# Filling products of a constant in place of identity transpositions, at the start of a clustered-attention and two-MLP kernel

## The chip, the cores and the metric

The kernel runs on one core of one Trainium2 chip. The metric is device time in microseconds (us) for one execution, lower being better. Before the change three runs took 782.43, 779.1 and 779.32 us: a median of 779.32 us. A further execution was recorded by the hardware profiler; the rows below come from that one.

## The reference

Three stages follow each other, all in float32. The first is attention in which a query sees only the keys of its own cluster; its output goes through one MLP with softplus, and that through a gated one with silu.

```python
q_assign = argmax(einsum('bhsd,hcd->bhsc', q_n, c_n), -1)   # q_n, k_n, c_n: normalised
k_assign = argmax(einsum('bhsd,hcd->bhsc', k_n, c_n), -1)
mask = q_assign[:, :, :, None] == k_assign[:, :, None, :]
scores = where(mask, q @ k.T / sqrt(D), -1e9)
x = softmax(scores) @ v            # B 2, H 8, S 768, D 64, 16 clusters
x = softplus(x @ w_in) @ w_out     # 1536 tokens, 512 -> 2048 -> 512
return (silu(x @ w_gate) * (x @ w_val)) @ w_out2    # 512 -> 1536 -> 512
```

The filling products that the change is about are no part of this: their result is never read.

## The kernel before, in words

Heads are taken in pairs; the 16 pieces of batch and head give 8 pairs, and each head has 6 blocks of 128 queries. One block is one step of the main loop: scores into PSUM (`sc`, L589), the row maximum on VectorE (L597), the exponential on ScalarE (L605), six transpositions of the probabilities on TensorE (`tr`, L621), their split into a high part (ScalarE, L627) and a low part (VectorE, L628), and the products with v (`pv`, L638). After the attention come the two MLPs (L914, L1092, L1185, L1435), nearly all of it TensorE work.

Ahead of the loop stands a prologue, written out by hand for the first pair. Each engine works off its own queue in the order in which the program issues it, so the order of the code is the order of the work:

- q and k of the first pair come in four pieces (`qkn`, L376), two halves each, on the queues of SP and ScalarE; the centroids (`cnc`) on SP's.
- TensorE has nothing to do until the first piece lands. It is filled with work whose result nobody reads: two products of a 128 x 128 tile of ones with itself (L390), then `warm(9)`, nine transpositions of the identity `id32` (L387). The identity is built by GpSimd (masks.py:197 and 199).
- `prep_x` (L455) transposes a half of q or k, three 128 x 128 transpositions; ScalarE or VectorE copies the result out (L463, L460, L465). The order on TensorE is: q half 0, `warm(1)`, k half 0, the centroids' transposition `cps` (L431), `warm(1)`, q half 1.
- `sims0` (L719) then multiplies the transposed q and k with the centroids `C`, 12 products with only 32 moving columns in two groups of six for each half; VectorE finds the cluster of each row (`arg0`, L732 to L737).
- The same is done for q of the next pair (`prep_x` L455, `sims_tile` L497), the cluster numbers are transposed (`hot_t`, L787), and the first scores are made (L589).

All of the filling writes the tile `warm_ps`, which is 128 columns of the PSUM bank with the tag "o". `prep_x` of q half 1 takes that bank next, so it waits until the last filling transposition is out of TensorE's pipeline.

The lines that the change touches:

```python
    warm_ps = ps_o.tile([128, 512], F32, tag="o", name="warm")[:, 0:128]
    ones = nc.const_aps.tensor(1.0, [128, 128], F32)

    def warm(n):
        for _ in range(n):
            nc.tensor.transpose(warm_ps, id32, id32)

    for _ in range(2):
        nc.tensor.matmul(warm_ps, lhsT=ones, rhs=ones, start=True, stop=True)
    warm(9)
```

Of the kernel before, what the change touches and what calls it, by code (L numbers as in the profile page):

```python
# [41 lines left out]
def kernel(  # L42
# [18 lines left out]
    nc = tc.nc  # L61
# [29 lines left out]
    id32 = keep.tile([128, 128], F32, name="id32")  # L91
# [290 lines left out]
    warm_ps = ps_o.tile([128, 512], F32, tag="o", name="warm")[:, 0:128]  # L382
    ones = nc.const_aps.tensor(1.0, [128, 128], F32)

    def warm(n):
        for _ in range(n):
            nc.tensor.transpose(warm_ps, id32, id32)  # L387

    for _ in range(2):
        nc.tensor.matmul(warm_ps, lhsT=ones, rhs=ones, start=True, stop=True)  # L390
    warm(9)

    nc.vector.tensor_copy(idr, id32)
    ohs = sml.tile([4 * C, 2], F32, name="ohs", bufs=1)
# [361 lines left out]
    bank_from(ps_t, "t")  # L756
    prep_x(0, 0, 0)
    warm(1)
    prep_x(0, 1, 0)
    centroid_blocks()  # L760
    warm(1)
    high0(0, 0)
    bank_from(ps_o, "o")
# [862 lines left out]
```

## Time and profile before

| | before |
|---|---|
| median of three runs | 779.32 us |
| the profiled execution's own time | 785.12 us |
| its span, first to last instruction | 783.3 us |
| TensorE busy (products / weight loads) | 779.0 / 714.4 us |
| VectorE, ScalarE, GpSimd busy | 614.0, 492.4, 171.2 us |
| granted TensorE clock, mean of the span | 0.991 |

A product's row in the timeline is a group of neighbouring instructions: start, time from the first one's start to the last one's end, engine, line, what it writes and reads, and how many. PE is the products, PEld the loads of the stationary operand ahead of them. A float32 product is two records in the trace, with a load each (two products of ones appear as x4); a float32 transposition is one. The time of one record contains the way through the pipeline, so records overlap: the step from one record to the next is (time of the group - time of its last record) / (count - 1). "Granted clock" is the share of TensorE's full 2.4 GHz that its throttle let through: 1.00 is 2.4 GHz and 0.50 is 1.2 GHz.

### The profile page before, as it was taken

The page shows a single profiled execution, that of the slowest core. Times are in us where ns is not written, and L with a number is a line of the kernel's source. Part 1 is how long each engine was busy: PE and PEld are TensorE (multiplying, and loading weights), DVE is VectorE, ACT ScalarE, POOL GpSimd, SP SyncE. Part 2 cuts the span into 40 slices and gives each one's busy share as a digit, 9 for nine tenths or more (in the row PEclk, how much of TensorE's full clock was granted, in tenths as well). Part 3 has the DMA queues.
Part 4 walks back from the last instruction along what each step waited for, and adds up shares of the span by engine and source line. Part 5 has one row for each costly group of instructions (what it writes and reads, how often), then busy time and mean ns, then how long its engine had stood idle before and what let it go on. Part 6 is the DMA issues. An engine that isn't in the chain of part 4 may idle for free.

```text
span 783.3 us, 12198 instructions
## 1 busy us (share of the span) xinstructions
PE 779.0 (99%) x4542; PEld 714.4 (91%) x4542; DVE 614.0 (78%) x988; ACT 492.4 (63%) x893; POOL 171.2 (22%) x174
## 2 busy tenths in 40 slices
PE   9999999999999999999999999999999999999998
PEld 9999999999999888889889898899999999999996
DVE  5899988988998798888776777998756766665664
ACT  5889889889897465447456465366564555555430
POOL 9545556556533000100100100000001011101100
PEclk7999999999999999999999999999999999999999
DMA  8784864864611323725736525113336567667554
GB/s 204 202 216 127 207 159 123 190 156 122 144 32 48 112 81 107 189 55 133 142 104 131 111 78 188 54 63 99 123 147 139 121 143 154 142 115 151 87 185 162
DMA packets 72652, 102.80 MB, mean 131 GB/s; under 512 B 29808, under 2 KB 52688, under 8 KB 72592
## 3 DMA queue, kind: packets, MB, share of 16 engines
q1 hardware_dynamic: 66608, 82.94, 36.1%
q0 software_dynamic: 5184, 18.88, 15.9%
q8 instruction: 36, 0.59, 0.3%
q10 hardware_dynamic: 800, 0.20, 0.1%
q14 instruction: 24, 0.20, 0.1%
HBM read 52.99 MB, written 26.79 MB: 102 GB/s over the span
## 4 chain that ended last, share of the span: by engine, by line
PE 93%; DVE 4%; ACT 1%; DMA 1%; issue 0%; SPq 0%; DVEq 0%
PE x L1185 17%; PE ob L1092 17%; PE ob L1435 12%; PE w L1185 9%; PE sps L589 8%; PE ops L638 8%; PE tps L621 8%; PE bank L914 5%; PE y L1185 4%; PE sims L497 2%; PE mps L455 2%; DVE tl L628 1%; DMA R<-rd 1%; DVE gl L1010 0%; ACT th L627 0%; PE mps L555 0%
## 5 line engine op out<-in xcount | busy, mean ns | idle before, releaser
L628 DVE TENSOR_TENSOR tl<-tps,th 128x384 fp32r<-128x384 f32 x192 | 98.1, 550 | 8.6 <-ACT th L627 7.5
L597 DVE TENSOR_REDUCE nm<-sps 128x1 f32<-128x768 f32 x96 | 91.2, 950 | 12.5 <-PE sps L589 10.7
L627 ACT CAST th<-tps 128x384 fp32r<-128x384 f32 x192 | 84.7, 491 | 16.4 <-PE tps L621 13.2
L621 PE MATMUL tps<-id,p 128*128 128x128 f32 x576 | 92.4, 280 | 0.1
L605 ACT ACTIVATE p<-sps,nm 128x768 f32<-128x768 f32 x96 | 88.1, 918 | 2.9 <-DVE nm L597 2.9
L589 PE MATMUL sps<-KT,QT 128*128 128x384 f32 x384 | 85.5, 345 | 0.0
L621 PEld LDWEIGHTS tps<-id,p 128*128 128x128 f32 x576 | 74.4, 150 | 8.0 <-DVE tl L628 3.5
L638 PE MATMUL ops<-th,VV 128*128 128x256 f32 x288 | 80.0, 307 | 0.0
L1452 POOL DMA_DIRECT2D out_dram<-side x21 | 18.1, 863 | 275.5 <-ACT side L1448 275.5
L638 PE MATMUL ops<-tl,VV 128*128 128x256 f32 x288 | 72.6, 282 | 0.0
L589 PEld LDWEIGHTS sps<-KT,QT 128*128 128x128 f32 x384 | 64.8, 194 | 0.0
L1435 PE MATMUL ob<-whi,aa 128*128 128x512 f32 x168 | 56.7, 391 | 0.0
L175 DVE TENSOR_TENSOR wlo<-m,whi 128x512 fp32r<-128x512 f32 (+1 forms) x63 | 38.6, 625 | 21.4 <-ACT whi L170 21.1
L638 PEld LDWEIGHTS ops<-th,VV 128*128 128x128 f32 x288 | 54.4, 189 | 0.4 <-DVE xu L659 0.2
L638 PEld LDWEIGHTS ops<-tl,VV 128*128 128x128 f32 x288 | 54.7, 190 | 0.0
L1118 POOL DMA_DIRECT2D far_acc<-side x15 | 13.1, 870 | 189.0 <-ACT side L1113 189.0
L170 ACT CAST whi<-m 128x512 fp32r<-128x512 f32 (+1 forms) x62 | 34.0, 561 | 29.5 <-DVE m L154 29.4
L1092 PE MATMUL ob<-gl,whi 128*128 128x512 f32 x168 | 51.9, 390 | 0.1
L1092 PE MATMUL ob<-gh,whi 128*128 128x512 f32 x168 | 51.8, 390 | 0.0
L1092 PE MATMUL ob<-gh,wlo 128*128 128x512 f32 x168 | 51.8, 389 | 0.0
L175 DVE TENSOR_TENSOR wlo<-side,whi 128x512 fp32r<-128x512 f32 x30 | 20.7, 692 | 31.6 <-ACT whi L170 31.5
L154 DVE SCALAR_TENSOR_TENSOR m<-raw,m 128x512 int32<-128x512 int32 x68 | 44.7, 686 | 0.7
(281 smaller groups left out, 1973.4 us busy)
## 6 DMA issues: line engine op xcount, KB each, us to landing
raw<-in_moe_w_out_dram SPq DMA_DIRECT2D x28, 512.0 KB, 4.4
out_dram<-side POOLq DMA_DIRECT2D x21, 512.0 KB, 5.6
raw<-in_moe_w_in_dram SPq DMA_DIRECT2D x16, 512.0 KB, 4.4
far_acc<-side POOLq DMA_DIRECT2D x15, 512.0 KB, 6.0
raw<-in_moe_w_gate_dram SPq DMA_DIRECT2D x12, 512.0 KB, 3.5
raw<-in_moe_w_val_dram SPq DMA_DIRECT2D x12, 512.0 KB, 4.2
QT<-hi SPq DMA_DIRECT2D x30, 192.0 KB, 3.5
KT<-hi SPq DMA_DIRECT2D x14, 384.0 KB, 6.0
```

Of the source, the lines that this page charges most:

```text
L154: nc.vector.scalar_tensor_tensor(out=m, in0=lo, scalar=29, in1=m, op0=ALU.logical_shift_right, op1=ALU.bitwise_or)
L175: low()
L589: nc.tensor.matmul(ps[:, c, 0:384], lhsT=Q[:, a, 128 * j:128 * j + 128], rhs=K[:, a, 384 * c:384 * c + 384], start=(a == 1), stop=(a == 0),)
L597: nc.vector.tensor_reduce(out=nm, in_=ps[:, :, 0:384], axis=AX.XY, op=ALU.max, negate=True)
L605: nc.scalar.activation(out=_h(p), in_=s_t.pop(i)[:, :, 0:384], func=AF.Exp, bias=nm_t.pop(i), accum_out=sm_t[pr][:, j:j + 1],)
L621: nc.tensor.transpose(ps[:, 128 * j:128 * j + 128], p[:, 128 * kb:128 * kb + 128], id32)
L627: nc.scalar.copy(th, pv)
L628: nc.vector.tensor_tensor(out=tl, in0=pv, in1=_r(th), op=ALU.subtract)
L638: nc.tensor.matmul(o[:, 0:CW], lhsT=VV_t[pr][:, hh, kb].rearrange("p a d -> p (a d)"), rhs=t[:, kb, :], start=(kb == 0 and lohi == 0), sto ...
L1092: nc.tensor.matmul(bk[:, t, :], lhsT=wt[:, 0, 128 * d:128 * d + 128], rhs=gt[:, 512 * c:512 * c + 512], start=(ends[0] and ff == 0 and n = ...
L1185: nc.tensor.matmul(dst[:, c, :], lhsT=wt[:, at + kk, :], rhs=x(part, kk)[:, HT // 2 * c:HT // 2 * c + HT // 2], start=(first and kk == 0 a ...
L1435: nc.tensor.matmul(bk[:, t, :], lhsT=lhs[:, ts_], rhs=rhs[:, 0, :], start=(ff == 0 and i == 0), stop=(ff == 1 and i == 2),)
```

## The change

The two products of ones and the nine identity transpositions become 12 products of the same tile of ones with 64 of its columns, and `warm(1)`, which is called twice between the transpositions of q and k, becomes one such product each time. The stationary operand keeps its 128 columns; the moving one has 64 instead of 128. Everything behind moves up two lines in the code.

```diff
     def warm(n):
         for _ in range(n):
-            nc.tensor.transpose(warm_ps, id32, id32)
-
-    for _ in range(2):
-        nc.tensor.matmul(warm_ps, lhsT=ones, rhs=ones, start=True, stop=True)
-    warm(9)
+            nc.tensor.matmul(warm_ps[:, 0:64], lhsT=ones, rhs=ones[:, 0:64], start=True, stop=True)
+
+    warm(12)
```

TensorE's queue from its first product to q half 1, before the change (`warm` is the filling, `mps` a transposition of q or k, `cps` that of the centroids; in brackets the semaphores waited for, DMAHW being a landing):

```order
L390 MATMUL warm<-const-float32-1.0 128x128 x2
L387 MATMUL warm<-id_72 128x128 [waits Pool_49]
L387 MATMUL warm<-id_72 128x128 x8
L455 MATMUL mps<-id_72,qkn 128x128 [waits DMAHW2_49,DMAHW0_49]
L455 MATMUL mps<-id_72,qkn 128x128 x2
L387 MATMUL warm<-id_72 128x128
L455 MATMUL mps<-id_72,qkn 128x128 [waits DMAHW4_49,DMAHW3_49]
L455 MATMUL mps<-id_72,qkn 128x128 x2
L431 MATMUL cps<-id_72,cnc_107 64x128 [waits DVE_49]
L387 MATMUL warm<-id_72 128x128
L455 MATMUL mps<-id_72,qkn 128x128 [waits DMAHW6_49,DMAHW5_49,PE_49]
```

Eleven filling instructions stand ahead of the first transposition of q, and the first identity transposition waits for GpSimd. The same stretch of TensorE's queue with the change:

```order
L387 MATMUL warm<-const-float32-1.0 128x64 x12
L453 MATMUL mps<-id_72,qkn 128x128 [waits DMAHW2_49,DMAHW0_49,Pool_49]
L453 MATMUL mps<-id_72,qkn 128x128 x2
L387 MATMUL warm<-const-float32-1.0 128x64
L453 MATMUL mps<-id_72,qkn 128x128 [waits DMAHW4_49,DMAHW3_49]
L453 MATMUL mps<-id_72,qkn 128x128 x2
L429 MATMUL cps<-id_72,cnc_107 64x128 [waits DVE_49]
L387 MATMUL warm<-const-float32-1.0 128x64
L453 MATMUL mps<-id_72,qkn 128x128 [waits DMAHW6_49,DMAHW5_49,PE_49]
```

Twelve products stand there now, and the wait for GpSimd's identity has moved to the first transposition of q. Nothing else in the queue has changed its place.

## Rows read from the trace of the kernel before

**Rows 1.** The page: span, busy time by engine, the chain that ended last by engine.

```profile
span 783.3 us, 12198 instructions
...
PE 779.0 (99%) x4542; PEld 714.4 (91%) x4542; DVE 614.0 (78%) x988; ACT 492.4 (63%) x893; POOL 171.2 (22%) x174
...
PE 93%; DVE 4%; ACT 1%; DMA 1%; issue 0%; SPq 0%; DVEq 0%
```

**Rows 2.** Timeline of the first 24 us, TensorE's rows in part.

```profile
0.79 1.19 PE L390 MATMUL warm<-const-float32-1.0 128*128 128x128 f32 x4 [0.79 <-PEq L1610]
1.77 2.13 PE L387 MATMUL warm<-id 128*128 128x128 f32 x9
...
3.82 0.50 PEld L455 LDWEIGHTS mps<-id,qkn 128*128 128x128 f32 x3 [0.32 <-issue]
...
6.07 0.55 PE L455 MATMUL mps<-id,qkn 128*128 128x128 f32 x3
...
6.45 1.42 PE L719 MATMUL y<-C,xr 128*128 128x32 f32 x12
...
9.59 1.52 PE L455 MATMUL mps<-id,qn 128*128 128x128 f32 x6
...
11.25 2.73 PE L497 MATMUL sims<-C,xr 128*128 128x32 f32 x12
...
18.05 2.60 PE L497 MATMUL sims<-C,xr 128*128 128x32 f32 x12
...
20.46 1.63 PE L589 MATMUL sps<-KT,QT 128*128 128x384 f32 x4
...
28.05 0.82 PE L621 MATMUL tps<-id,p 128*128 128x128 f32 x6
```

**Rows 3.** Instructions of L390, L387, L719, L497, L621: count, ns min/median/max, first and last start.

```profile
L390 PE MATMUL warm<-const-float32-1.0 x4: 421/422/553, 0.8 to 1.6; 128*128 128x128 f32 x4
L387 PE MATMUL warm<-id x11: 421/421/421, 1.8 to 5.6; 128*128 128x128 f32 x11
L719 PE MATMUL y<-C,xr x24: 195/276/389, 6.5 to 9.4; 128*128 128x32 f32 x24
L497 PE MATMUL sims<-C,xr x168: 193/276/402, 11.2 to 201.1; 128*128 128x32 f32 x168
L621 PE MATMUL tps<-id,p x576: 270/272/421, 21.9 to 248.2; 128*128 128x128 f32 x192
```

**Rows 4.** Windows: busy by engine, then granted clock, DMA share, GB/s.

```profile
core 0: us, PE busy (x) PEld busy (x) DVE busy (x) ACT busy (x) POOL busy (x), PEclk, DMA share, GB/s
0.00:6.00 6.00, 5.21 (x22) 4.49 (x22) 2.69 (x16) 2.44 (x5) 5.22 (x28) 1.00 0.62 139
6.00:9.40 3.40, 3.34 (x31) 3.25 (x31) 2.34 (x6) 2.74 (x7) 3.17 (x5) 1.00 0.96 221
9.40:23.06 13.66, 13.66 (x64) 13.47 (x63) 7.29 (x14) 7.17 (x15) 13.15 (x14) 0.50 0.96 264
23.06:26.50 3.44, 3.38 (x21) 2.44 (x20) 3.25 (x7) 3.36 (x9) 0.76 (x1) 1.00 0.94 256
```

**Rows 5.** Who TensorE's weight loads waited for, whole span, and in the first 30 us.

```profile
PEld tps L621 <- DVE tl L628: 3.5, 17, 0.4
...
PEld tps L621 <- DVE tl L628: 1.0, 4, 0.4
```

## The prediction

> **What bounds the kernel now.** I read the page first [rows 1]: TensorE is busy 779.0 of 783.3 us and is 93% of the chain that ended last. Time that TensorE loses anywhere is therefore time of the kernel, unless it waits for another engine soon after. That is nearly never so: its longest wait for one line is 3.5 us, for VectorE's L628, in 17 pieces over the whole span, 1.0 us of it in the first 30 us [rows 5]. So I take a delay at the start as passed through to the end, less what a later wait could swallow, at most 1 us near by.
>
> The change lies in the first 6 us, so I read the timeline there next [rows 2]. The filling starts at 0.79. The nine transpositions start at 1.77 and take 2.13 us with the pipeline's tail; without the last one's tail (421 ns for a record, a step of (2.13 - 0.42) / 8 = 0.213 us) the array is free at 1.77 + 9 x 0.213 = 3.69. The first load for q half 0 comes at 3.82. It waits for landings only, so the data was there at 3.8: **the filling ends 0.13 us before it is in the way.**
>
> Then the clock. The windows give the granted clock as 1.00 until 9.4, 0.50 from there to 23.06, and 1.00 after [rows 4]. The first value is not what ran. An identity transposition took 421 ns from 1.8 to 5.6 us, every one of the 11, and a transposition in L621 took 421 ns at most and 272 ns at the median [rows 3]; its step at 28.05 is (0.82 - 0.27) / 5 = 0.110 us [rows 2], half of 0.213. So TensorE ran at 1.2 GHz until about 6 us. From there the three transpositions at 6.07 fit in 0.55 us and the L719 records took 276 ns, which is 2.4 GHz. Read that way: half speed until 6, full for 3.4 us, half for 13.66 us, then full for good.
>
> What the engine did before each turn is what matters here. Ahead of the rise at 6 it ran 128-column transpositions almost without a gap. Ahead of the fall at 9.4 it ran mostly L719, products of 32 columns. In the half-speed stretch it ran L497 twice, again 32 columns. It rose at 23.06, after the scores at 20.46 and their transpositions, which follow the last L497.
>
> **The change part by part.**
>
> (1) The filling itself. Removed: 4 records of ones and 9 transpositions, 13 steps. Added: 12 products, 24 records of 64 moving columns, each with a weight load of 128 columns. No row shows 64 columns. The rows on both sides do, at 1.2 GHz: ones with 128 columns step by 0.213 us or a little more ((1.19 - 0.42) / 3 = 0.257 with the slow first one), and L497 with 32 columns by (2.73 - 0.40) / 11 = 0.212 [rows 2, 3]. Four times the columns, the same step: at these sizes the step is that of the weight load, which the change leaves as it is. So I take 0.213 for 64 columns. As a lower bound I keep half of it, 0.107, as if columns decided.
> 24 x 0.213 = 5.11, and 0.13 for the slow first record: the filling ends at 0.79 + 5.24 = 6.03 instead of 3.69, and q half 0 starts 6.03 - 3.82 = **2.2 us late**. At the lower bound it ends at 3.5 and costs nothing, the wait for data at 3.82 covering it.
>
> (2) The two single fillings: one record of 0.213 becomes two, **+0.43 us**. The second has no cover: q half 1 waits for the bank it writes. The first loses whatever cover the data of k half 0 gave it; that data has landed when q is 2.2 us late. Lower bound 0.
>
> (3) The wait for GpSimd's identity moves to q half 0. The old first transposition of it began at 1.77 [rows 2], so it is done 2 us ahead of the data: nothing. VectorE, ScalarE and SP have their orders unchanged; what they take from TensorE's first results comes later by the same 2 to 3 us. Behind them GpSimd is busy 13.15 of the 13.66 us from 9.4 [rows 4], but what it makes there (the second head's operands, v) is read by TensorE only from 26.5 on, and TensorE is later too.
>
> (4) The clock. The transpositions that came ahead of the rise at 6 are gone. In their place stand products with half their columns at the same step, so that the array is fed half as densely. 64 columns lie between the 128 ahead of a rise and the 32 ahead of a fall. I take it that the rise at 6 does not come, the nearer likeness being a step that is mostly weight load. Then the work from 6.07 to 9.59 (6 transpositions, 24 records of L719) runs at 1.2 GHz: 30 x 0.213 = 6.4 us instead of 3.5, **+2.9 us**. Lower bound 0, if the rise comes all the same.
> The Trainium skill says the opposite of what I read: in "TensorE: Matmul & The Clock Gate", Part 4, PE-mode transpose, the full clock does not engage for transpositions, as they don't count as busy in the same way. By that rule real products would be the better filling. The trace disagrees here: from 1.77 to 6 TensorE ran nothing but transpositions, and then came the full clock.
>
> (5) What comes back. TensorE reaches the transpositions of 9.59 at 2.2 + 0.4 + 2.9 = 5.5 us late. If the full clock comes at the same moment as before, 23.06, those last 5.5 us of work run at 2.4 GHz: -2.7. If it comes at the same point of the work, nothing comes back. If it comes later in the work, up to the 12 L497 records and 4 score products behind the first dense stretch (2.4 + 1.4 us at half speed), some 2.4 us more are lost with what follows. I see no row that ties it to a moment, and take -0.8, nearer to the same point of the work.
>
> Sum: 2.2 + 0.4 + 2.9 - 0.8 = **+4.7 us**. Made against the profiled execution that is 785.12 + 4.7 = 789.8 with the profiler on. That execution stands 5.8 us above the median of the plain runs, so for a plain run I put the sum on the median: 779.32 + 4.7 = **784.0 us**. The plain runs themselves differ by 3.3 us, which is about what an earlier or later rise of the clock is worth by (5).
>
> **The rivals.**
>
> *Columns decide the step.* 24 records at 0.107 end at 3.5, before the data, as the filling did before. For it: a real product of fewer columns streams less. Against it: 32 and 128 columns have one step in rows 2. Time: 779.3 if the clock rises as before, 779.3 + 2.9 = 782.2 if not. [...]
>
> *Products bring the clock up.* The filling is slow as in (1) until the full clock comes, at 6 or up to 2 us sooner. At 6: q half 0 is 2.2 us late; it, k and the single fillings then run at full speed, 11 steps of 0.110 instead of 0.213, which leaves 1.5 us (2.2 + 0.4 - 1.1) at q half 1; and 1.5 us of L719 is pushed behind the fall at 9.4 and costs as much again: 3.0, so 782.3. Sooner: some 10 of the 24 records at 0.110, so 1.0 less on the filling: about 780. For it: real products ran ahead of the rise at 6, too, from 0.79 to 1.98. Against it: these were four records, the rest transpositions.
>
> *Faster: products bring the clock up and it stays up.* Decided by the granted clock after 9.4: if it stays at 1.00, the 13.66 us of half speed shrink to 6.8 if VectorE and ScalarE, 7.3 and 7.2 us busy there [rows 4], can follow: about -6.5, less 2 us of late filling, 774.8. Against it: L719 and L497 are untouched, and the clock fell during the one and stayed low over the other.
>
> **How the numbers follow.** A measurement of this kernel can tell about 0.5% from no change, 3.9 us here: 775.4 to 783.2 counts as the same. My forecast has a chance of 0.60, with its own range from 781.3 (2.0, the full 2.7 coming back and some of 2 covered) to 787.2 (5.5 and 2.4 more); four fifths of it lie over 783.2, 0.48. Columns decide: 0.14, counted with the same. Products bring the clock up: 0.18, 0.04 of it slower. It stays up: 0.06, faster; 0.02 more for a lucky early rise. Together: faster 0.08, same 0.40, slower 0.52. The range of 778.0 to 787.2 leaves out the faster case and a tenth or so at the top.
>
> **What would show it.** In the profile of the changed kernel: 24 filling records with a step of 0.21 us, ending near 6.0; the first q transposition at 6.0 and not 3.85; L719 with records of about 0.40 us and its first row near 9.2; the first L455 of `qn` near 15 instead of 9.59; no full clock between 6 and 9.4. Wrong in (1) if the first q load still comes at 3.8; wrong in (4) if L719's median stays at 276 ns; wrong as a whole if the clock is up before the first score product.

## The result: slower by 8.6 us, and the profile after

The changed kernel took 787.13, 787.55, 788.16 and 790.38 us, a median of 787.86, against 779.21 before (four runs on the same chip). The ratio is 1.0102, 95% interval 1.0069 to 1.0134: slower, with the whole interval above the 0.5% that the prediction took as telling. The forecast was slower by 4.7 to 784.0 with a range up to 787.2; the way was right, the time lies 0.7 us above the range.

The timeline of the changed kernel's first 29 us, TensorE's rows in part, against [rows 2]:

```profile
0.79 5.35 PE L387 MATMUL warm<-const-float32-1.0 128*128 128x64 f32 x24 [0.79 <-PEq L1608]
5.93 0.85 PE L453 MATMUL mps<-id,qkn 128*128 128x128 f32 x3
6.57 0.53 PE L387 MATMUL warm<-const-float32-1.0 128*128 128x64 f32 x2
6.89 0.85 PE L453 MATMUL mps<-id,qkn 128*128 128x128 f32 x3
...
7.74 0.53 PE L387 MATMUL warm<-const-float32-1.0 128*128 128x64 f32 x2
8.33 0.90 PE L453 MATMUL mps<-id,qkn 128*128 128x128 f32 x3
9.02 2.61 PE L717 MATMUL y<-C,xr 128*128 128x32 f32 x12
...
14.54 1.52 PE L453 MATMUL mps<-id,qn 128*128 128x128 f32 x6
...
16.19 2.73 PE L495 MATMUL sims<-C,xr 128*128 128x32 f32 x12
...
19.65 1.63 PE L587 MATMUL sps<-KT,QT 128*128 128x384 f32 x4
...
21.57 1.20 PE L587 MATMUL sps<-KT,QT 128*128 128x384 f32 x4
22.61 1.42 PE L495 MATMUL sims<-C,xr 128*128 128x32 f32 x12
...
28.89 0.36 PE L636 MATMUL ops<-th,VV 128*128 128x256 f32 x1
```

24 filling records step by (5.35 - 0.42) / 23 = 0.214 us and are through at 5.93, where the first transposition of q now starts instead of 3.85. Twelve L717 records take 2.61 us where they took 1.42, and the `qn` transpositions come at 14.54 instead of 9.59. The first sign of the full clock is inside the group at 21.57: 1.20 us where the same four products took 1.63 at 19.65. The instructions of the two lines say the same:

```profile
L387 PE MATMUL warm<-const-float32-1.0 x28: 314/421/443, 0.8 to 7.8; 128*128 128x64 f32 x28
L717 PE MATMUL y<-C,xr x24: 261/401/401, 9.0 to 14.3; 128*128 128x32 f32 x24
```

The median of L717 is 401 ns after 276 before [rows 3]. The granted clock does not show any of this. The windows of the changed kernel's trace read 1.00 from the start:

```profile
core 0: us, PE busy (x) PEld busy (x) DVE busy (x) ACT busy (x) POOL busy (x), PEclk, DMA share, GB/s
0.00:6.00 6.00, 5.21 (x25) 5.25 (x26) 2.32 (x15) 1.78 (x3) 5.22 (x28) 1.00 0.62 139
6.00:9.40 3.40, 3.34 (x18) 3.12 (x17) 1.41 (x2) 1.55 (x5) 1.36 (x3) 1.00 0.96 218
9.40:22.10 12.70, 12.70 (x62) 12.60 (x62) 5.51 (x13) 6.54 (x13) 10.70 (x12) 1.00 0.69 179
22.10:26.50 4.40, 4.25 (x32) 3.89 (x31) 3.90 (x7) 3.64 (x8) 4.20 (x5) 1.00 0.99 319
```

By the durations TensorE ran at 1.2 GHz for 22 us. The windows before the clock's first turn can't be relied on, then: here, as in the first 6 us of the kernel before [rows 4], they print 1.00 over half speed. A likely reason, not shown, is that nothing is recorded ahead of the first turn. The page still shows a span that is TensorE's from end to end:

```profile
span 786.4 us, 12224 instructions
...
PE 781.2 (99%) x4555; PEld 717.3 (91%) x4555; DVE 614.4 (78%) x988; ACT 493.0 (63%) x893; POOL 171.3 (22%) x174
...
PE 96%; DVE 1%; ACT 1%; DMA 1%; issue 0%
```

One thing does not fit: the span grew by 3.1 us only (783.3 to 786.4), the plain median by 8.6. So the recorded execution of before may not have been one of its usual ones.

### The profile page after: what moved, and what is told of

Its sections match the earlier page's. It is cut to its first block, busy times and chain, and to the rows that moved or that the text cites. A ratio compares the mean times of both kernels' runs of the same rounds, so it can differ in the third digit from the quotient of the medians.

```text
span 786.4 us, 12224 instructions
## 1 busy us (share of the span) xinstructions
PE 781.2 (99%) x4555; PEld 717.3 (91%) x4555; DVE 614.4 (78%) x988; ACT 493.0 (63%) x893; POOL 171.3 (22%) x174
## 4 chain that ended last, share of the span: by engine, by line
PE 96%; DVE 1%; ACT 1%; DMA 1%; issue 0%
PE x L1183 17%; PE ob L1090 17%; PE ob L1433 12%; PE w L1183 8%; PE ops L636 8%; PE sps L587 8%; PE tps L619 8%; PE bank L912 8%; PE y L1183 4%; PE sims L495 2%; PE mps L453 1%; PE bank L936 1%; PE warm L387 1%; DMA QT<-OH 1%; PE y L717 1%; DVE tl L626 0%
## 5 line engine op out<-in xcount | busy, mean ns | idle before, releaser
L625 ACT CAST th<-tps 128x384 fp32r<-128x384 f32 x192 | 84.7, 491 | 14.2 <-PE tps L619 11.5
```

What stands on the lines that cost most here:

```text
L625: nc.scalar.copy(th, pv)
```

## The experiments

The theories. **A**: a float32 filling product steps with its load of stationary columns, so the filling ends 2 us late; and behind these products, with half the moving columns in each step, the full clock does not come up early, as it does behind filling with 128 columns. **Rivals**: only the late filling costs; only real products bring the clock up; columns decide the step; the turns of the clock stand at fixed times. The kernels were timed in three groups, each with before beside it: 77 executions of before, with medians of 779.37, 779.08 and 779.63 us.

**b_again: before once more.** No edit.

> The kernel before, unchanged, with a second profile. Theory A (the turns of the clock do not stand at fixed times after the start, and where they fall makes the 778.7 to 782.4 us of the plain runs): the median is 779 to 782, and the profile shows the rise, the fall and the last rise at other times than 6.0, 9.4 and 23.06 us. Rival B (the turns are fixed, and the profiler itself makes the difference to 785): the three turns are within 0.3 us of those times.

Measured: 779.56 us over 10 executions from 778.74 to 785.84; 1.0007 (0.9975 to 1.0039). The new profile has a span of 777.0:

```profile
4.16 0.59 PE L455 MATMUL mps<-id,qkn 128*128 128x128 f32 x3 [0.26 <-DMA qkn<-in_q_dram]
...
6.00 1.42 PE L719 MATMUL y<-C,xr 128*128 128x32 f32 x12
...
9.04 0.85 PE L455 MATMUL mps<-id,qn 128*128 128x128 f32 x6
...
10.14 1.52 PE L497 MATMUL sims<-C,xr 128*128 128x32 f32 x12
...
12.05 0.98 PE L589 MATMUL sps<-KT,QT 128*128 128x384 f32 x4
...
20.54 0.36 PE L638 MATMUL ops<-th,VV 128*128 128x256 f32 x1
```

Here the 12 records of L497 take 1.52 us and not 2.73 [rows 2]: the full clock came up ahead of 5 us and did not fall at 9.4 at all. The three transpositions at 4.16 already take 0.59 us, where those at half speed take 0.85 or more. The first `pv` product (L638) is at 20.54; in the recorded execution of before it was at 26.54. Rival "fixed times" is out. The recorded execution, with a mean of 0.991, was one of a minority in which the clock falls for a while: the mean granted clock of the ten was 0.989 in the two at 785.5 and 785.8 us, 0.996 in the two at 782.4 and 782.6, and 0.999 or 1.000 in the six at or below 779.8. Of the 77 executions of before, 24 took over 781 us.

**e1_five: five products instead of twelve.**

```diff
-    warm(12)
+    warm(5)
```

> 5 products of 64 columns in place of 12, the single ones as in the change. Theory A: 10 records of 0.213 us end at about 3.0, so q half 0 starts at 3.8 to 3.9 as before the change, but there is no full clock around 6 to 9.4 and L717 has records of 401 ns. Against the change 2.1 us less: about 785.5, and still 4 to 7 above before. Rival B (the late filling alone costs, the clock does not matter): 779 to 780.

Measured: 785.12 us, 1.0071 (1.0056 to 1.0087), 2.7 below the change.

```profile
0.79 2.37 PE L387 MATMUL warm<-const-float32-1.0 128*128 128x64 f32 x10 [0.79 <-PEq L1608]
3.96 0.88 PE L453 MATMUL mps<-id,qkn 128*128 128x128 f32 x3 [0.80 <-DMA qkn<-in_q_dram]
...
7.08 2.61 PE L717 MATMUL y<-C,xr 128*128 128x32 f32 x12
...
19.63 1.13 PE L587 MATMUL sps<-KT,QT 128*128 128x384 f32 x4
```

The filling is over 0.8 us before the data, L717 still runs at half speed, and 5.7 us of the 8.6 are still there. "The late filling alone" is out.

**e2_wide: the change with 128 columns.**

```diff
-            nc.tensor.matmul(warm_ps[:, 0:64], lhsT=ones, rhs=ones[:, 0:64], start=True, stop=True)
+            nc.tensor.matmul(warm_ps, lhsT=ones, rhs=ones, start=True, stop=True)
```

> The change with 128 moving columns in place of 64. Theory A: the step stays 0.213 us, q half 0 starts 1 to 2.2 us late, but the full clock comes at some time up to 7 us and most of L717 has records of 276 ns: 781 to 784. Rival B (what the moving columns are does not matter to the clock): no full clock before 16 us, 787 to 790 as the change. Rival C (columns decide the step): the step is well above 0.213.

Measured: 781.01 us, 1.0015 (1.0005 to 1.0024), all ten from 779.5 to 781.66.

```profile
0.79 5.46 PE L387 MATMUL warm<-const-float32-1.0 128*128 128x128 f32 x24 [0.79 <-PEq L1608]
6.04 0.68 PE L453 MATMUL mps<-id,qkn 128*128 128x128 f32 x3
...
8.04 1.42 PE L717 MATMUL y<-C,xr 128*128 128x32 f32 x12
```

Twice the columns cost 0.1 us: 24 records are through at 6.04 instead of 5.93. So in this row the step is not set by the columns that stream. But L717 runs at full speed behind them. With the filling just as late, the kernel is 1.6 us above before where the clock comes up, and 8.6 where it does not.

**e3_ids: transpositions only.** The filling of before with no product of ones, 21 identity transpositions at the outset and two in each single place.

```diff
-    for _ in range(2):
-        nc.tensor.matmul(warm_ps, lhsT=ones, rhs=ones, start=True, stop=True)
-    warm(9)
+    warm(21)
...
-    warm(1)
+    warm(2)
...
-    warm(1)
+    warm(2)
```

> 21 transpositions of the identity, and two at a time where the change has one product, with no product of ones at all: the filling ends where that of the change does, at about 5.9. Theory A (dense transpositions bring the clock up by themselves): the full clock comes by 7 us, q half 0 at most 2.2 us late, 781 to 784, as with 128 columns. Rival B (only products count, as the Trainium skill has it in TensorE: Matmul & The Clock Gate, Part 4): no full clock before 16 us, 787 to 790.

Measured: 780.93 us, 1.0017 (1.0002 to 1.0032).

```profile
1.37 4.70 PE L387 MATMUL warm<-id 128*128 128x128 f32 x21 [1.37 <-POOL id masks.py:199]
5.91 0.49 PE L453 MATMUL mps<-id,qkn 128*128 128x128 f32 x3
...
7.71 1.42 PE L717 MATMUL y<-C,xr 128*128 128x32 f32 x12
```

Three transpositions in 0.49 us at 5.91: full speed, with nothing but transpositions ahead. The Trainium skill's statement in "TensorE: Matmul & The Clock Gate", Part 4, PE-mode transpose, that the full clock does not engage for them, does not hold for these float32 transpositions; the measurement decides.

**e4_six: six products of 128 columns**, two records in each single place. The edit is that of e2_wide with `warm(6)`.

> Six products of 128 columns ahead of the data, and one such at each of the two single places. Theory A (a filling with 128 columns that ends before the data costs nothing and brings the clock up): 12 records of 0.213 us end at 3.5, q half 0 starts at 3.8 to 4.2, the full clock comes between 4 and 7 us; 778.7 to 780.5. Rival B (real products of a constant bring less than transpositions do): no full clock before 16 us, 784 to 786.

Measured: 779.28 us, 1.0001 (0.9978 to 1.0025).

```profile
0.79 2.90 PE L387 MATMUL warm<-const-float32-1.0 128*128 128x128 f32 x12 [0.79 <-PEq L1608]
3.67 0.56 PE L453 MATMUL mps<-id,qkn 128*128 128x128 f32 x3
...
6.67 1.42 PE L717 MATMUL y<-C,xr 128*128 128x32 f32 x12
```

The 12 records are through when q half 0 starts, at 3.67, and L717 takes 1.42 us. Behind real products of a constant with 128 columns the clock came up here as it does behind the transpositions of before. In one execution of the ten, at 786.14 us, the mean granted clock was 0.991, as in the recorded one of before.

**e5_square: 64 stationary columns too.**

```diff
-            nc.tensor.matmul(warm_ps[:, 0:64], lhsT=ones, rhs=ones[:, 0:64], start=True, stop=True)
+            nc.tensor.matmul(warm_ps[0:64, 0:64], lhsT=ones[:, 0:64], rhs=ones[:, 0:64], start=True, stop=True)
```

> The products of the change with 64 stationary columns as well as 64 moving ones. Theory A (the load of the stationary columns sets the step, and a stream with half the columns in half the step is as dense as before): a step of 0.107 us, 24 records end at 3.4, q half 0 at 3.8 to 4.2, the full clock by 7 us; 778.7 to 781. Rival B (the step is fixed per float32 record, whatever the columns): 0.213 us, q half 0 at 5.9, 787 to 788. Rival C (the step halves but a product of 64 columns does nothing for the clock): q half 0 on time, no full clock before 16 us, 784.5 to 785.5.

Measured: 779.5 us, 1.0018 (0.9988 to 1.0047), seven executions from 778.98 to 779.77 and three from 785.25 to 787.0. The profile caught one of the three:

```profile
0.79 2.79 PE L387 MATMUL warm<-const-float32-1.0 128*64 128x64 f32 x24 [0.79 <-PEq L1608]
3.70 0.87 PE L453 MATMUL mps<-id,qkn 128*128 128x128 f32 x3
...
7.18 2.61 PE L717 MATMUL y<-C,xr 128*128 128x32 f32 x12
```

The step is (2.79 - 0.31) / 23 = 0.108 us, with 314 ns for a record (its median in this trace): half the stationary columns, half the step. With e2_wide this shows that in a long row of such products the stationary columns set the step, not the moving ones. That it is their load, and not something else that goes with them, is the likely reading but was not tested apart. On the clock the kernel is mixed. In seven of ten its time is that of before, so there the clock most likely came up early, though none of the seven was profiled; in the profiled one it did not. So the early rise can come behind products of 64 columns (rival C, as stated, falls), but why in some executions and not in others was not settled.

**e6_none: no filling at all.** All three calls of `warm` are removed.

> No filling at all, neither the 12 products nor the two single ones. Theory A (the filling of the change does nothing for the clock): q half 0 at 3.8 to 4.2, no full clock before 16 us, 784 to 785.5, that is 2.5 to 4 us below the change. Rival B (half as dense a filling is still worth something): above the change or level with it, 787 to 789.

Measured: 784.49 us, 1.0077 (1.005 to 1.0103): 784.08, 784.47, 784.51 and 788.25. The profile is of the last, the one that stands apart:

```profile
3.81 1.53 PE L452 MATMUL mps<-id,qkn 128*128 128x128 f32 x6 [3.81 <-DMA qkn<-in_q_dram]
...
6.41 2.61 PE L716 MATMUL y<-C,xr 128*128 128x32 f32 x12
...
27.92 1.25 PE L586 MATMUL sps<-KT,QT 128*128 128x384 f32 x4
```

q half 0 starts at 3.81, and L716, which is L717 of the change, takes 2.61 us. The full clock comes only inside the group at 27.92 here, which may be what sets this execution apart; the three others have no profile. By the medians the filling of the change is 3.4 us worse than none, or 2.6 with the median of after_again; that of before is 5.4 us better than none.

**e7_single: the two single fillings alone.** The filling of before, with a product of 64 columns in place of each single transposition.

> The filling of the kernel before at the outset, and only the two single transpositions replaced by products of 64 columns. Theory A: at most 0.4 us more than before, 779 to 780, with the full clock by 7 us. Rival B (the two single ones take the clock down): 784 to 786.

Measured: 782.72 us, 1.0037 (1.0013 to 1.0062): neither theory. Six of ten executions were over 781 us, against 5 of the 24 of before beside them. The profile is one of the six; the clock rises near 6 and falls near 9.3, as in the recorded one of before. The first single product costs 0.1 us more than a transposition: k half 0 starts 0.31 us behind it (4.62 to 4.93 in this profile), where the step after a transposition is 0.21. Beside the before of its group the kernel is slower, with an interval that lies above 1. Whether the single products also make the fall more frequent, or whether ten executions are too few, stays open: over all three groups before had 24 of 77.

**after_again: the changed kernel once more.**

> The changed kernel, unchanged, with a second profile. Theory A: the step is 0.213 us again, q half 0 starts at 5.9, and the full clock first comes between 19 and 25 us, wherever it falls in the work; 787 to 790. If the wait of L587 for the transfer QT<-OH (1.1 us in the first profile) belongs to the change, it is there again; if it was chance, it is not, and the time is the same within 1 us or so.

Measured: 787.11 us over nine executions, 781.81 to 789.25; 1.0061 (1.0026 to 1.0096). The filling, L717 and the rise stand as in the first profile within 0.02 us, and the first `pv` product is at 28.88, there 28.89. The first profile also had this row among the waits of TensorE's loads, at the change of a head pair near 106 us:

```profile
PEld sps L587 <- DMA QT<-OH: 1.1, 1, 1.1
```

The second does not have it, and its span is 785.3, just 1.1 less. It is not part of the change. Three of the nine took 781.8 to 784.7 us. None of them was profiled; by their times the full clock came earlier there. So the change most likely does not shut the early rise out in every execution.

**e8_seven and e9_pairs: two tries at a better one.** e8_seven is e4_six with `warm(7)`; e9_pairs is before with `warm(2)` in both single places.

> Seven products of 128 columns instead of six, the single ones as there. Theory A (a filling that reaches up to the data leaves no hole before q half 0, and so loses the full clock in fewer executions): 14 records end at 3.9, at most 0.2 us late; 778.8 to 779.8, and fewer executions above 781 than the kernel before has. Rival B (what decides is where the clock's turns fall, not the hole): the same share of executions above 781, a fifth or so.

> The kernel before with two identity transpositions at each of the two single places. Theory A (denser single fillings hold the full clock through L719 more often): the median 0.1 to 0.4 us above before, 779.1 to 779.8, with fewer executions above 781. Rival B (they only cost): 779.3 to 780 and a fifth of the executions above 781 as before.

Measured: e8_seven 780.35 us, 1.0013 (0.9991 to 1.0036), 4 of 12 over 781 us; e9_pairs 779.3 us, 0.9991 (0.996 to 1.0021), 2 of 12 over 781, with before at 779.63 and 12 of 28. Neither can be told from before. With a third of its executions over 781 us, e8_seven gives no sign of its theory A; the share of e9_pairs goes the way of its own, but 12 executions are too few to show it. No version was found that beats before.

## Why the prediction was right, and where it fell short

Where the lateness builds up, against the usual execution of before (the profile of b_again) and against the recorded one:

| start of | usual before | recorded before | after | late against usual / recorded |
|---|---|---|---|---|
| q half 0 | 4.16 | 3.85 | 5.93 | 1.8 / 2.1 |
| first products with the centroids | 6.00 | 6.45 | 9.02 | 3.0 / 2.6 |
| `qn` transpositions | 9.04 | 9.59 | 14.54 | 5.5 / 5.0 |
| first score product | 12.05 | 14.70 | 19.65 | 7.6 / 5.0 |
| first `pv` product | 20.54 | 26.54 | 28.89 | 8.4 / 2.4 |
| end (span) | 777.0 | 783.3 | 786.4 | 9.4 / 3.1 |

Of the last row 1.1 us is the wait for QT<-OH, which after_again did not have. Rows of the recorded before that the table and the steps rest on, beside [rows 2]:

```profile
3.85 0.87 PE L455 MATMUL mps<-id,qkn 128*128 128x128 f32 x3
4.52 0.42 PE L387 MATMUL warm<-id 128*128 128x128 f32 x1
4.73 0.85 PE L455 MATMUL mps<-id,qkn 128*128 128x128 f32 x3
...
5.59 0.42 PE L387 MATMUL warm<-id 128*128 128x128 f32 x1
...
14.70 1.63 PE L589 MATMUL sps<-KT,QT 128*128 128x384 f32 x4
...
26.54 0.36 PE L638 MATMUL ops<-th,VV 128*128 128x256 f32 x1
```

- Step (1), the filling: right. 0.213 us was taken for a record, 0.214 was measured; the end at 6.03 was forecast, 5.93 measured (the first record was less slow). e2_wide and e5_square bear out the reason given: the stationary columns set the step.
- Step (2), +0.43 for the single ones: half of that. The pair at 6.57 puts k half 0 0.32 us behind its start, where one transposition at 4.52 put it 0.21 behind; the second place takes 0.59 us (7.74 to 8.33) after 0.48 (5.59 to 6.07). That is 0.11 each, +0.21 in all: the second record of such a pair follows the first by 0.53 - 0.42 = 0.11 us, not by the 0.213 of the long row.
- Step (3), nothing for the moved wait: right. q half 0 follows the filling without a gap. One reading in it was not: GpSimd's work from 9.4 to 23.06 begins with low parts of QT and KT (L754, until 11.28 us), which the score products from 14.70 on read. It had no effect, as no score product waited for GpSimd in the first 30 us of either trace.
- Step (4), no full clock at 6 to 9.4: right. L717 has 401 ns, and from q half 1 to the `qn` transpositions TensorE takes 6.21 us (8.33 to 14.54) after 3.52 (6.07 to 9.59): +2.7, where 2.9 was taken. The sum of (1), (2) and (4) was 5.5 at the `qn` transpositions. Against the recorded execution, from which it was worked out, it is 2.1 + 0.2 + 2.7 = 5.0. The 5.5 against the usual one is luck: there q half 0 starts later, and the clock rises sooner.
- **Step (5) failed**: "I see no row that ties it to a moment, and take -0.8". It assumed that before loses the clock at 9.4 in any case, as the one recorded execution did, so that from there on the change had only something to get back; and it then put the sum on the median of the plain runs, in most of which the clock stays up. Against the recorded execution something did come back, and more than was taken: 28.89 - 14.54 = 14.35 us to the first `pv` product after 26.54 - 9.59 = 16.95, or -2.6, close to the -2.7 named for a rise at the same moment. In the usual execution, though, the same work takes 20.54 - 9.04 = 11.5 us; after the change the first 7.5 us of it run at half speed, until 22 us. Against the median the term is +2.9, not -0.8, and 5.5 + 2.9 = 8.4 is the measured 8.6 but for 0.2.
- What the late rise goes by stayed open. In the profiles of e1_five and e5_square it falls in the same group of score products as in the change, which starts 1.9 us earlier there (19.63 and 19.73, after 21.57): there it went with the work. In that of e6_none it came three blocks of queries later.

The warning was in the text: the recorded execution stood 5.8 us above the plain median, and this was put down to the profiler. It should have been asked what in the kernel can be 5.8 us longer in one execution. The half-speed stretch of 13.66 us [rows 4] was a candidate of that size, half of it being 6.8, and the two profiles of before do differ by 6.3 us in their span. Had it been taken as the exception, a loss by half speed would have stood in place of the -0.8; how large, no row of before could tell.

Of the rivals, "columns decide the step" fell with e2_wide and e5_square, and "products bring the clock up" with the profiles of the change and of after_again, and by their times with ten of the 13 executions. "It stays up" named the right thing for the wrong kernel: the clock does stay up through L719 and L497, but in the kernel before.

The parts, by medians: filling that ends late costs 2.7 us at half speed (the change against e1_five) or 1.6 at full speed (e2_wide against before); the lost clock costs 5.4 (e6_none against before) or 6.9 (the change against e2_wide), more there probably as the late work is itself done at half speed. The change stands in these at its 787.86; with the 787.11 of after_again, 2.7 becomes 2.0 and 6.9 becomes 6.1. That the moving columns decide is shown by the change against e2_wide, which differ in nothing else; why the narrower products leave the clock low in most executions is not.

## What to carry to other kernels

Price a row of small float32 products by their stationary columns before their moving ones; halving the latter saved nothing in the long row here, and behind it the full clock came late in most executions. Filling is worth its time only while nothing waits for it: count its records up to the landing of the first data. And when a profiled execution is longer than the plain runs, look for the stretch that makes it so, before a sum is built on it.

## What the runs showed that was not expected

Where the clock turns is not a fixed property of a kernel: of 87 executions of before (77 and the ten of b_again) 28 took over 781 us, in two groups. Eighteen took 781.2 to 783.8 us, all but one of them with mean granted clocks of 0.993 to 0.997, and ten 785.4 to 786.9 with 0.989 to 0.991. The granted clock of a trace can mislead before its first turn: the changed kernel shows 1.00 for 22 us at half speed, and its mean of 1.000 is higher than the 0.991 of the recorded execution of before, which was faster. Durations of one record (421 or 272 ns for a float32 transposition) tell the two apart. And in a long row, float32 products with 128 stationary columns step by 0.21 us a record at the lower clock, with 32, 64 or 128 moving columns, and by 0.108 with 64 stationary ones; in a pair by itself the second record of 64 moving columns follows after 0.11.
